# The projections and the FFN of a two-layer transformer as matmuls of 32 output columns, with the pace table searched anew

## The chip, the core and the metric

The kernel runs on one core of one Trainium2 chip. The metric is the device time of one execution in microseconds. The time before is 803.99 us, the median of 3 runs (803.82 to 804.15). The profile comes from one more execution with the hardware profiler on.

The engines that matter are TensorE (PE: matmuls into PSUM; PEld is its weight load), ScalarE (ACT: exponentials), VectorE (DVE) and GpSimd (POOL) for elementwise work, and SyncE (SP), which issues most of the DMAs.

## What is computed

Two blocks, each applied twice with the same weights, to x of 1 x 2048 x 448 in bf16. Block A is softmax attention with 16 heads of 28 columns, block B a feed-forward network with a squared relu.

```python
def _A_ref(x, wqkv, wo):
    B, S, D = x.shape
    H = 16; Dh = D // H
    qkv = (x @ wqkv).reshape(B, S, 3, H, Dh).transpose(2, 0, 3, 1, 4)
    q, k, v = qkv[0], qkv[1], qkv[2]
    scores = jnp.einsum("bhqd,bhkd->bhqk", q, k) * Dh ** -0.5
    p = _softmax(scores, axis=-1)
    o = jnp.einsum("bhqk,bhkd->bhqd", p, v)
    return o.transpose(0, 2, 1, 3).reshape(B, S, D) @ wo

def _B_ref(x, w1, b1, w2, b2):
    h = jnp.einsum("bsd,df->bsf", x, w1) + b1
    r = jnp.where(h > 0, h, 0)
    return jnp.einsum("bsf,fd->bsd", r * r, w2) + b2

x = A_x
x = x + _A_ref(_layernorm(x), A_wqkv, A_wo)
x = x + _B_ref(_layernorm(x), B_w1, B_b1, B_w2, B_b2)
x = x + _A_ref(_layernorm(x), A_wqkv, A_wo)
x = x + _B_ref(_layernorm(x), B_w1, B_b1, B_w2, B_b2)
```

The transposes are written here in plain form; the hidden width F is 1792.

## The kernel before

**Tiling.** The 448 columns of x stand in four chunks of 128 rows (the last is half zero). Each head is padded to 32 columns, so four heads make a group of 128 rows and 16 heads make four groups. Queries are worked off in blocks of 256 (two token tiles of 128); the last two blocks of the second layer have 128. Keys come in tiles of 128.

**Scores.** A score unit is one head's 512 scores per partition: two key tiles by 256 queries, or four by 128. There are 2048 units. A score group (`s_stream`, L1150) holds three units, each a matmul that uses 32 rows of PE and all 128 columns; units of different heads use different rows and run side by side. The group is written to one of two PSUM buffers of three banks (`sc`).

**Exponentials.** ACT takes a whole group with one instruction (`e_stream`, L1188). For some groups the third unit is taken away and given to DVE, so that ACT's instruction has two units (128 x 1024) in place of three (128 x 1536). DVE builds the exponential from bit operations in `a_unit`: a first pass at L1210 or L1212 that reads the scores. After L1210 the rest stays on DVE (L1228, L1232, L1235). After L1212 come three half passes (L1259, L1265, L1270), each on POOL or DVE, and a closing product on DVE (L1274).

**Value sums.** The exponentials of a key tile are multiplied by V (`p_stream`, L1376, and L1341 for units of DVE). These matmuls use all 128 rows of PE and 32 output columns, one head each; four heads, with four weight loads and four moving operands, run side by side into the four quarters of the partitions of one PSUM tile (`oT`).

**Projections and FFN.** All dense products go through one helper, `mm_tile`, with its matmuls at L805: K, Q and V (`qkv`), the output projection with `wo`, the hidden layer with `w1` and the FFN's output with `w2` (all three in `chain`). Each is a matmul of 128 rows by 128 output columns. The moving operand has N=256 columns (K, Q, `w1`), N=128 (the same for the blocks of 128 queries), N=448 (V, `wo`, `w2`), or N=320 and 128 at the very end. `mm_tile` cuts a tile's list of matmuls into operations of at most some 0.46 us (`MMC`), so that scores can come between. Each operation carries a mode, and `mm_tile` leaves it at its default, `"full"`.

**The order of the work.** The order on every engine is fixed when the program is built. `Planner.run` holds a list of streams with priorities, keeps a planned clock for every engine, and always emits the operation that can start first, scores ahead of other work. It counts 0.1 us when PE goes from one mode to another (row for scores, col for value sums, full for the rest):

```python
if e == "PE" and self.mode != o.mode:
    s = max(t, self.clock[e] + 0.1)
```

It also fills: a score group can be computed again (`again` in `s_stream`), and `heat` (L1625) adds matmuls whose result nobody reads, both when the planned load of PE over the last few microseconds is low (`HEAT`, `WINDOW`, `HOT`). The load is counted with a weight per mode:

```python
USE = {"row": 0.7, "col": 0.98, "full": 0.93}
```

**The pace.** Whether a group gives its third unit to DVE is decided in `apart`, by limits on DVE's planned load and backlog (`BUSY`, `LOW`, `TB`, `TB2` and others). `PACE` is a table that sets these and other planner constants anew when a given score group is reached, and `FORCE` and `SKIP` list groups that give the unit away, or don't, whatever the limits say.

Of the kernel before, what the change touches and what calls it, by code (L numbers as in the profile page):

```python
# [17 lines left out]
DHP = 32  # L18
G = 4
# [11 lines left out]
PLIM = 99.0  # L31
# [3 lines left out]
LADD = 0.15  # L35
NCELL = 9
RES = 2
RES2 = 4
XMIN = 4
HELD = 0.14  # L40
PWAIT = 3.0
# [52 lines left out]
NEAR = 3  # L94
# [17 lines left out]
AEND = 1  # L112
HOT = 0.9
MORE = 1
HEAT = 0.45
HWIN = 3.4
NEAR_U = 0
LASTP = 3.2
# [24 lines left out]
MMC = 0.46  # L143
VGAP = 0.03
QP = 6
FORCE = (22, 27, 31, 36, 64, 104, 108, 120, 122, 156, 162, 192, 196, 233, 235, 237, 254, 263, 287, 292, 301, 306,
         329, 341, 392, 408, 430, 445, 466, 501, 515, 553, 556, 567, 577, 593, 598, 602)
SKIP = (20, 29, 46, 135, 184, 195, 216, 222, 242, 262, 280, 282, 320, 321, 378, 388, 395, 404, 406, 409, 416, 418,
        433, 440, 446, 479, 500, 512, 526, 544, 574, 601, 609, 621, 622, 646, 652, 663)
PACE = {  # L150
    0: {'BUSY': 0.95, 'LOW': 0.7, 'CHUNK': 1, 'EV': 2.9, 'FAR': 6, 'KEEP': 5, 'LAG': 8, 'LEAD': 18, 'MARGIN': 3,
         'MORE': 3, 'PRE': 0.5, 'SLACK': 0.7, 'SPAN': 8, 'TB': 2.4, 'TB2': 2.4, 'V_AGE': 5, 'V_LAST': 3, 'V_PAST':
         2, 'C_PRIO': 1.6, 'V_PRIO': 4, 'V_LATE': 2.6, 'V_WAIT': 5, 'ASIDE': 1, 'XMIN': 4, 'HOLD': 6, 'LADD': 0.05,
         'RES': 2, 'RES2': 2, 'TASIDE': -0.2, 'EPRIO': 2.6, 'SPARE': 0, 'NEAR': 3, 'SOON': 1, 'VGAP': 0.03, 'PWAIT':
         0.3, 'PNEAR': 0.2, 'PORTP': 1, 'PLIM': 99.0},
    8: {'LEAD': 12, 'BUSY': 0.9, 'PLIM': 2},
    16: {'SPAN': 11},
    24: {'LAG': 3},
    32: {'PLIM': 2.6, 'EV': 3.5},
    40: {'TB2': 3.0},  # L160
    42: {'BUSY': 0.95, 'CHUNK': 3, 'EV': 2.9, 'LAG': 8, 'LEAD': 18, 'MORE': 1, 'SPAN': 8, 'TB': 1.6, 'TB2': 2.4,
         'V_PRIO': 8.5},
    56: {'BUSY': 1.0, 'LAG': 3},
    64: {'NEAR': 9, 'ASIDE': 0.2, 'LADD': 0.1},
    72: {'V_AGE': 4},
    88: {'V_AGE': 3},
    112: {'C_PRIO': 1.2, 'HOLD': 5},
    120: {'LEAD': 10, 'LAG': 12, 'SPARE': 3, 'ASIDE': 2},
    128: {'TB': 2.0, 'MORE': 3},
    136: {'PRE': 1.2, 'MARGIN': 6},  # L170
    144: {'EPRIO': 4},
    152: {'CHUNK': 1, 'VGAP': 0},
    160: {'BUSY': 0.95, 'V_PRIO': 4, 'V_PAST': 3},
    168: {'RES': 1, 'C_PRIO': 2.1, 'LOW': 1.0},
    176: {'EV': 2.2, 'TB2': 2.0, 'LOW': 0.5},
    192: {'PORTP': 0.3, 'SOON': 0.6},
    200: {'CHUNK': 2, 'PRE': 0.3},
    208: {'PNEAR': 0.25, 'V_AGE': 6},
    216: {'NEAR': 3},
    248: {'EPRIO': 6},  # L180
    256: {'ASIDE': 0},
    264: {'MARGIN': 10},
    280: {'PORTP': 2},
    288: {'HOLD': 6},
    296: {'TB': 1.0, 'PNEAR': 0.15},
    304: {'SPAN': 6},
    312: {'BUSY': 1.0},
    320: {'LEAD': 12, 'MARGIN': 6},
    328: {'V_LATE': 6},
    336: {'LOW': 1.0},  # L190
    360: {'PNEAR': 0.05, 'TB': 2.4, 'V_LATE': 2.6, 'V_AGE': 3},
    368: {'C_PRIO': 1.6},
    376: {'PNEAR': 0.15, 'V_PRIO': 8.5},
    384: {'XMIN': 3, 'LEAD': 18},
    392: {'CHUNK': 3},
    400: {'KEEP': 6, 'ASIDE': 4, 'V_AGE': 6, 'BUSY': 0.9},
    408: {'PWAIT': 0.6, 'MORE': 1},
    424: {'RES': 2, 'BUSY': 1.0},
    440: {'HEAT': 0.6, 'WINDOW': 3.4, 'CHUNK': 2},
    456: {'V_AGE': 5, 'TB': 1.3},  # L200
    480: {'TB': 1.6, 'PORTP': 0.3, 'PLIM': 2},
    488: {'LADD': 0.2, 'HOLD': 4},
    496: {'MARGIN': 3, 'PNEAR': 0.35},
    504: {'PWAIT': 0.3},
    512: {'KEEP': 4, 'EV': 2.9},
    520: {'V_AGE': 4, 'C_PRIO': 1.2, 'HOLD': 5},
    528: {'PRE': 0.8},
    536: {'XMIN': 4, 'SPAN': 15, 'ASIDE': 2, 'PRE': 0.3},
    544: {'V_AGE': 5, 'EV': 2.2},
    552: {'PORTP': 1, 'LEAD': 12, 'FAR': 17, 'PRE': 0},  # L210
    560: {'V_LATE': 6, 'VGAP': 0.03},
    568: {'SPARE': 0, 'NEAR': 9},
    576: {'SOON': 1.5, 'PNEAR': 0.15},
    584: {'PLIM': 1.3, 'LAG': 3, 'V_WAIT': 3},
    592: {'KEEP': 6, 'V_LAST': 2.2},
    600: {'V_AGE': 8},
    608: {'EV': 1.3, 'LOW': 0.8},
    616: {'PRE': 1.2, 'BUSY': 0.95, 'V_PAST': 2, 'FAR': 6},
    624: {'LADD': 0.1, 'BUSY': 0.9},
    648: {'PRE': 0.5, 'SPAN': 20, 'EV': 3.5, 'ASIDE': 0.2},  # L220
    656: {'ASIDE': 1, 'SLACK': 0.4},
    672: {'SOON': 1, 'ASIDE': 0.2},
    680: {'SLACK': 0.7},
}


# [180 lines left out]
def kernel(  # L407
# [205 lines left out]
    def pools_now(early=False):  # L613
        return (*R_m, R_sc) if early and ("s", LEND) not in pl.tok or len(s_left) == 0 else R_m
# [169 lines left out]
    def mm_tile(subs, evac, ev_dur, deps, any_engine=False, sets=(), early=False, post=(), acq=None, alone=0, seen=None, across=False):  # L784


        box = {}
        mms = [(c0, n, lhsT, rhs, i == 0, i == len(ops) - 1, own)
               for c0, n, ops in subs for i, (lhsT, rhs, *own) in enumerate(ops)]
        if across:  # L790
            mms = [mms[k * len(subs[0][2]) + i] for i in range(len(subs[0][2])) for k in range(len(subs))]
            mms = [(*m[:4], m is mms[0], m is mms[-1], m[6]) for m in mms]
        first = last = None
        i = 0
        while i < len(mms):
            dur, k = 0.003, i
            while k < len(mms) and (k == i or dur + mms[k][1] / 2400 < (0.6 if i == 0 and alone else MMC) and not (alone and k == alone)):
                dur += max(0.07, mms[k][1] / 2400 + 0.003)
                k += 1

            def fn(e, part=mms[i:k], i=i):
                if i == 0:
                    box["t"] = bank(first, "mt")
                for c0, n, lhsT, rhs, a, b, _ in part:
                    nc.tensor.matmul(box["t"][:, c0:c0 + n], lhsT=lhsT() if callable(lhsT) else lhsT, rhs=rhs,  # L805
                                     start=a, stop=b)
# [872 lines left out]
```

## Time and profile before

| | |
|---|---|
| median of 3 runs | 803.99 us (803.82 to 804.15) |
| the profiled execution | 804.07 us |
| its span, first to last instruction | 802.3 us |
| mean granted clock of PE | 1.000 |
| matmuls | 12234 |
| exponentials on ACT | 683 |

The span lies 1.8 us below the execution's own time; the rest is around the instructions. The profile's page has busy times, the chain that ended last, groups of instructions by line and the DMA queues. Besides the page, the trace answers with groups by shape, with waits (who waited for whom), with busy time by stretch, and with a timeline in which neighbouring instructions of one kind are merged: its columns are start and length in microseconds, engine, line, operation, tiles, shapes and count, and in brackets the idle time before. A matmul's recorded length holds its way through the array, so neighbouring matmuls overlap in the timeline; the distance of their starts is what they cost. "32\*128 32x256" means 32 rows and 128 columns of the array, a moving operand of 32 partitions and 256 columns.

### The profile page before, as it was taken

To read this page: it belongs to the slowest core of one execution; us is meant where nothing else is said; L and a number is where in the kernel's file an instruction comes from. 1 tells how busy PE (TensorE), PEld (TensorE's weight loads), DVE (VectorE), ACT (ScalarE), POOL (GpSimd) and SP (SyncE) were. 2 spreads that over 40 slices of the span, in tenths; PEclk is the share of its full clock that TensorE was granted. 3 is DMA by queue.
4 is the path that set the end of the run, shared out by engine and by line. 5 is a ranking of instruction groups with operands and counts; after the bars stand their busy time and mean duration, and the time that the engine had idled before them with its cause. 6 is when DMAs were issued, how large, how long until landed. Compare 5 with 4: busy or idle time off the path is not lost.

```text
span 802.3 us, 29224 instructions
## 1 busy us (share of the span) xinstructions
PE 779.4 (97%) x12234; PEld 417.7 (52%) x12234; DVE 744.6 (93%) x1818; ACT 789.6 (98%) x702; POOL 453.1 (56%) x715
## 2 busy tenths in 40 slices
PE   9999989999999999999999999989999999999998
PEld 6555545544555555555555545445454544546666
DVE  8999999999999999999999998999999999989554
ACT  9999999999999999999999999999999999999994
POOL 3446777657675664544566657667665576654100
PEclk9999999999999999999999999999999999999999
DMA  9300010000000000000000000011100000000000
GB/s 247 89 2 2 5 34 23 17 16 16 17 3 16 16 16 16 3 16 15 2 3 2 3 2 2 17 30 30 34 10 22 21 28 21 22 23 9 22 8 19
DMA packets 32336, 18.02 MB, mean 22 GB/s; under 512 B 17802, under 2 KB 31755, under 8 KB 32204
## 3 DMA queue, kind: packets, MB, share of 16 engines
q1 hardware_dynamic: 32060, 16.04, 7.3%
q8 instruction: 95, 1.56, 0.8%
q14 instruction: 37, 0.30, 0.1%
q10 hardware_dynamic: 144, 0.11, 0.0%
HBM read 13.87 MB, written 2.06 MB: 20 GB/s over the span
## 4 chain that ended last, share of the span: by engine, by line
PE 41%; ACT 31%; DVE 17%; issue 8%; DMA 1%; POOL 0%; SPq 0%; ACTq 0%; POOLq 0%; DVEq 0%
ACT pt L1188 31%; PE mt L805 19%; PE sc L1150 12%; PE oT L1376 7%; DVE pt L1212 3%; DVE r L1569 2%; PE oT L1341 1%; PE sc L805 1%; DVE V_sb L1576 1%; DVE pt L1210 1%; DVE v_c L1212 1%; DVE v_c L1274 1%; DVE K_sb L1274 1%; DVE x_sb L1509 1%; DVE K_sb L1212 1%
## 5 line engine op out<-in xcount | busy, mean ns | idle before, releaser
L1188 ACT ACTIVATE pt<-sc 128x1536 bf16<-128x1536 f32 (+1 forms) x683 | 776.8, 1289 | 1.2 <-PE sc L1150 0.9
L1150 PE MATMUL sc<-Q_sb,K_sb 32*128 32x256 bf16 (+1 forms) x4640 | 279.4, 265 | 15.9 <-ACT pt L1188 13.5
L1150 PEld LDWEIGHTS <-K_sb 32*128 32x128 bf16 x4640 | 100.9, 92 | 186.5 <-issue 118.5
L1376 PE MATMUL oT<-pt,V_sb 128*32 128x256 bf16 (+1 forms) x4000 | 167.7, 268 | 0.5 <-DVE Q_sb L824 0.3
L1376 PEld LDWEIGHTS <-V_sb 128*32 128x32 bf16 x4352 | 101.5, 96 | 45.3 <-issue 35.9
L805 PE MATMUL mt<-xnT,w 128*128 128x256 bf16 (+1 forms) x896 | 119.1, 271 | 0.9 <-DVE xnT L720 0.2
L1270 POOL TENSOR_SCALAR pt<-pt 128x512 int16<-128x512 int8 x131 | 84.2, 644 | 39.6 <-ACT pt L1188 5.7
L805 PEld LDWEIGHTS <-w 128*128 128x128 bf16 x952 | 78.0, 98 | 35.3 <-issue 26.6
L1212 DVE TENSOR_SCALAR pt<-sc 128x512 int16<-128x512 f32 x132 | 89.9, 684 | 2.3 <-PE sc L1150 1.6
L1569 DVE TENSOR_SCALAR r<-mt 128x512 bf16<-128x512 f32 (+1 forms) x107 | 73.1, 683 | 3.7 <-PE mt L805 3.2
L671 POOL TENSOR_TENSOR rstd<-mv,mhalf 128x2 f32<-128x2 f32 (+1 forms) x34 | 25.4, 748 | 79.2 <-DVE mv L674 72.7
L805 PE MATMUL mt<-w,V_sb 128*128 128x448 bf16 (+1 forms) x274 | 64.6, 348 | 0.0
L1270 POOL TENSOR_SCALAR v_c<-v_c 128x512 int16<-128x512 int8 x64 | 42.8, 668 | 24.5 <-DVE V_sb L1265 4.3
L1265 POOL TENSOR_SCALAR v_c<-pt 128x512 f16<-128x512 uint8 x57 | 38.1, 669 | 31.9 <-DVE K_sb L1259 5.8
L1509 DVE TENSOR_TENSOR x_sb<-x_sb,mt 128x448 bf16<-128x448 bf16 (+1 forms) x61 | 37.0, 607 | 13.2 <-PE mt L805 12.8
L1212 DVE TENSOR_SCALAR v_c<-sc 128x512 int16<-128x512 f32 x69 | 46.7, 683 | 0.7 <-PE sc L1150 0.6
L648 DVE BATCH_NORM_STATS2 st<-x_sb 128x6 f32<-128x448 bf16 x62 | 38.3, 619 | 0.6 <-DMA x_sb<-in_A_x_dram 0.5
L805 PEld LDWEIGHTS <-V_sb 128*128 128x128 bf16 x302 | 25.1, 98 | 24.9 <-issue 10.0
L1341 PE MATMUL oT<-v_c,V_sb 128*32 128x256 bf16 (+1 forms) x298 | 35.0, 273 | 0.0
L1270 POOL TENSOR_SCALAR K_sb<-K_sb 128x512 int16<-128x512 int8 x39 | 25.3, 649 | 11.2 <-DVE v_c L1274 2.5
L1265 POOL TENSOR_SCALAR K_sb<-pt 128x512 f16<-128x512 uint8 x35 | 23.9, 681 | 13.2 <-DVE pt L1212 4.3
L1576 DVE TENSOR_TENSOR V_sb<-r 128x512 bf16<-128x512 bf16 x70 | 29.2, 422 | 2.2 <-ACT r L1567 1.9
(217 smaller groups left out, 1257.4 us busy)
## 6 DMA issues: line engine op xcount, KB each, us to landing
rec<-scr SPq DMA_DIRECT2D x54, 128.0 KB
out_dram<-x_sb SPq DMA_DIRECT2D x15, 112.0 KB
x_sb<-in_A_x_dram SPq DMA_DIRECT2D x7, 224.0 KB
w<-in_B_w_dram SPq DMA_DIRECT2D x1, 1568.0 KB
w<-in_B_w_dram SPq DMA_DIRECT2D x1, 1344.0 KB
dn<-oT_sb SPq DMA_DIRECT2D x54, 4.0 KB
V_sb<-in_A_wqkv_dram SPq DMA_DIRECT2D x4, 168.0 KB
scr<-dn SPq DMA_DIRECT2D x27, 8.0 KB
```

The lines of the kernel that those rows point to most:

```text
L648: nc.vector.bn_stats(out=box["st"][:, :], in_=x_sb[:, t0 + j, :] if src is None else src())
L805: nc.tensor.matmul(box["t"][:, c0:c0 + n], lhsT=lhsT() if callable(lhsT) else lhsT, rhs=rhs, start=a, stop=b)
L1150: nc.tensor.matmul(dst[k][:, i * nt * P:(i + 1) * nt * P], lhsT=K_sb[l][rows, g, (kb + i) * P:(kb + i + 1) * P], rhs=Q_sb[rows, g, t0 * P: ...
L1188: t = nc.scalar.activation(out=pt[:, 0:n], in_=gbuf[gi]["sc"][:, 0:n], func=AF.Exp, scale=float(np.log(2.0)) * 2.0 ** -FRAC)
L1212: t = nc.vector.tensor_scalar(out=z.bitcast(DT.int16), in0=src, scalar1=2.0, scalar2=EXP_BIAS, op0=ALU.mult, op1=ALU.add)
L1265: on(e).tensor_scalar(out=box["f"], in0=gbuf[gi]["z"].bitcast(DT.uint8).rearrange("p (n t) -> p n t", t=2)[:, :, 0], scalar1=2.0 ** -9, sc ...
L1270: on(e).tensor_scalar(out=gbuf[gi]["z"].bitcast(DT.int16), in0=gbuf[gi]["z"].bitcast(DT.int8).rearrange("p (n t) -> p n t", t=2)[:, :, 1], ...
L1341: nc.tensor.matmul(box["t"][DHP * hh:DHP * hh + DHP, 0:n], lhsT=V_sb[l][:, kb + i, 4 * g + hh, :], rhs=gbuf[gi]["x2"][:, i * n:(i + 1) * n ...
L1376: nc.tensor.matmul(box["t"][DHP * hh:DHP * hh + DHP, 0:n], lhsT=V_sb[l][:, tb, 4 * g + hh, :], rhs=p, start=begin and j < G, stop=close an ...
L1509: nc.vector.tensor_tensor(out=x_sb[:, tb, lo:hi], in0=x_sb[:, tb, lo:hi], in1=t[:, 0:hi - lo], op=ALU.add)
L1569: nc.vector.tensor_scalar(out=r[:, 0:w], in0=t[:, 0:w], scalar1=0.0, scalar2=None, op0=ALU.max)
L1576: nc.vector.tensor_tensor(out=h[:, 0:w // n, :], in0=r, in1=r, op=ALU.mult)
```

## The change

The matmul in `mm_tile` becomes four, each with a quarter of the weight's columns and a quarter of the output's partitions, and the operation's mode becomes `"col"`:

```diff
                 for c0, n, lhsT, rhs, a, b, _ in part:
-                    nc.tensor.matmul(box["t"][:, c0:c0 + n], lhsT=lhsT() if callable(lhsT) else lhsT, rhs=rhs,
-                                     start=a, stop=b)
+                    w = lhsT() if callable(lhsT) else lhsT
+                    for c in range(G):
+                        nc.tensor.matmul(box["t"][DHP * c:DHP * c + DHP, c0:c0 + n],
+                                         lhsT=w[:, DHP * c:DHP * c + DHP] if len(w.shape) == 2 else w[:, c, :], rhs=rhs,
+                                         start=a, stop=b, tile_position=(0, DHP * c))
             own = list({d for m in mms[i:k] for d in m[6]})
             last = Op("PE", dur, fn, deps=(list(deps) if i == 0 else [last]) + own,
-                      acq=None if i else pools_now(early) if early else spare(len(mms)))
+                      acq=None if i else pools_now(early) if early else spare(len(mms)), mode="col")
```

`G` is 4 and `DHP` is 32. The planned length of an operation (`dur`) is not touched. Transposes and `heat` stay as they are.

Two constants and the pace are new. The tables `FORCE` and `SKIP` get other groups (29 and 26 in place of 38 and 38), and `PACE` other entries:

```diff
-WINDOW = 2.8
+WINDOW = 3.4
...
-HEAT = 0.45
+HEAT = 0.55
...
 PACE = {
-    0: {'BUSY': 0.95, 'LOW': 0.7, 'CHUNK': 1, 'EV': 2.9, 'FAR': 6, 'KEEP': 5, 'LAG': 8, 'LEAD': 18, 'MARGIN': 3,
-         'MORE': 3, 'PRE': 0.5, 'SLACK': 0.7, 'SPAN': 8, 'TB': 2.4, 'TB2': 2.4, 'V_AGE': 5, 'V_LAST': 3, 'V_PAST':
+    0: {'BUSY': 0.95, 'LOW': 0.7, 'CHUNK': 3, 'EV': 2.9, 'FAR': 6, 'KEEP': 5, 'LAG': 8, 'LEAD': 18, 'MARGIN': 3,
+         'MORE': 3, 'PRE': 0.5, 'SLACK': 0.7, 'SPAN': 8, 'TB': 3.4, 'TB2': 2.4, 'V_AGE': 5, 'V_LAST': 3, 'V_PAST':
...
-         'RES': 2, 'RES2': 2, 'TASIDE': -0.2, 'EPRIO': 2.6, 'SPARE': 0, 'NEAR': 3, 'SOON': 1, 'VGAP': 0.03, 'PWAIT':
+         'RES': 2, 'RES2': 2, 'TASIDE': 1, 'EPRIO': 2.6, 'SPARE': 0, 'NEAR': 3, 'SOON': 1, 'VGAP': 0.03, 'PWAIT':
...
-    8: {'LEAD': 12, 'BUSY': 0.9, 'PLIM': 2},
+    8: {'EV': 1.5, 'BUSY': 0.85, 'XMIN': 3},
...
```

As the planner decides all orders, the order on every engine is different behind the first groups of scores. Line numbers fall by 14 to 17: L805 becomes L790, L1150 L1136, L1188 L1174, L1376 L1362.

More of the change, by code (lines that the diff above doesn't have):

```diff
@@ L160 @@
[L160 to L201, printed above, removed]
@@ new lines @@
+    64: {'PLIM': 2, 'KEEP': 4},
+    80: {'C_PRIO': 1.2},
+    96: {'BUSY': 1.06, 'EV': 2.2},
+    104: {'V_PAST': 5},
+    112: {'LOW': 1.0},
+    128: {'RES2': 6, 'NEAR': 9},
+    136: {'NEAR': 3},
+    160: {'LOW': 0.5},
+    184: {'RES2': 4, 'MARGIN': 6},
+    192: {'V_LAST': 2.5},
+    200: {'VGAP': 0},
+    224: {'MARGIN': 10},
+    232: {'LAG': 12},
+    240: {'PNEAR': 0.35},
+    264: {'VGAP': 0.06},
+    272: {'VGAP': 0.15},
+    296: {'RES2': 2},
+    304: {'TASIDE': 0.2},
+    312: {'RES2': 6, 'V_LAST': 3},
@@ new lines @@
+    328: {'PORTP': 0},
+    336: {'PRE': 1.2},
+    344: {'SPARE': 3},
+    376: {'PNEAR': 0.25},
+    384: {'TASIDE': -0.2, 'FAR': 12},
+    400: {'NEAR': 9},
+    408: {'V_LAST': 2.5},
+    416: {'TASIDE': 0.2},
+    424: {'PORTP': 0.3, 'NEAR': 3},
+    440: {'CHUNK': 1},
+    464: {'VGAP': 0},
+    496: {'CHUNK': 2},
+    504: {'V_AGE': 8},
+    520: {'V_WAIT': 7, 'LOW': 0.7},
+    528: {'PRE': 0.3},
+    536: {'TB2': 0.9},
+    560: {'PLIM': 1.2},
+    568: {'V_LAST': 2.2},
+    576: {'LOW': 0.5},
```

45 lines of the change are left out of this document (16 added, 29 removed).

## The prediction

> **What bounds the kernel now.** I read the page first: the busy times, then the chain that ended last.
>
> ```profile
> PE 779.4 (97%) x12234; PEld 417.7 (52%) x12234; DVE 744.6 (93%) x1818; ACT 789.6 (98%) x702; POOL 453.1 (56%) x715
> ...
> PE 41%; ACT 31%; DVE 17%; issue 8%; DMA 1%; POOL 0%; SPq 0%; ACTq 0%; POOLq 0%; DVEq 0%
> ```
>
> No engine alone explains the time: ACT, PE and DVE are each over 90% busy, and the chain goes to and fro between them. So I cut the span into stretches and asked for the busy time of each. The columns are the stretch, its length, then busy microseconds and instructions of PE, PEld, DVE, ACT and POOL.
>
> ```profile
> 9.30:20.00 10.70, 10.70 (x104) 6.24 (x103) 10.53 (x30) 10.13 (x8) 1.68 (x4) 1.00 1.03 290
> 20.00:780.00 760.00, 741.71 (x11713) 391.09 (x11713) 719.75 (x1739) 759.38 (x671) 446.38 (x699) 1.00 0.06 17
> ...
> 787.30:802.30 15.00, 11.94 (x156) 9.34 (x153) 6.51 (x18) 4.84 (x9) 0.56 (x1) 1.00 0.06 17
> ```
>
> From 20 to 780 us ACT is busy 759.38 of 760.00 us: it works off exponentials without a pause, and the span is their sum plus about 9 us ahead of the first and 15 us behind the last. A change pays there if it takes exponentials from ACT, or loses if it makes one start late. How late they start now is in the waits (total us, times, longest):
>
> ```profile
> PE sc L1150 <- ACT pt L1188: 13.5, 31, 0.7
> ACT pt L1188 <- PE sc L1150: 0.9, 3, 0.5
> ```
>
> Of 683 score groups only 31 had to wait until ACT gave a buffer back. In all other places PE came to the scores from other work, so PE runs nearly as full as ACT and has little to give. ACT visibly waited three times. Small lateness is hidden in the recorded length of an exponential, so 0.9 us is a lower bound.
>
> **The change part by part.**
>
> *The exponentials left on ACT.* The pace decides which of the 2048 score tiles go to ACT and which to DVE. In the built order ACT has 345 exponentials of three tiles and 338 of two before, 341 and 342 after: 1711 tiles become 1707. The groups by shape give the price:
>
> ```profile
> L1188 ACT ACTIVATE pt<-sc 128x1536 bf16<-128x1536 f32 x345 | 489.7, 1501 | 0.6 <-PE sc L1150 0.5
> L1188 ACT ACTIVATE pt<-sc 128x1024 bf16<-128x1024 f32 x338 | 337.9, 1073 | 0.6 <-PE sc L1150 0.4
> ```
>
> The two differ by 1501 - 1073 = 428 ns, the cost of a tile; the number of instructions, and with it the fixed part, stays 683. Four tiles are 4 x 0.428 = 1.7 us less on an engine that has no pause. This lies wholly on the path: -1.7 us.
>
> *The four narrow matmuls.* Each of the 1254 matmuls of the projections and the FFN (L805) becomes four with 32 output columns. The shape with N=256 stands in the trace as the value sums (oT). First eight groups of four, then eight full matmuls, each up to the scores that follow (columns: start, length):
>
> ```profile
> 300.36 0.78 PEld L1376 LDWEIGHTS <-V_sb 128*32 128x32 bf16 x32 [0.21 <-issue]
> 300.36 0.28 PE L1376 MATMUL oT<-V_sb,V_sb 128*32 128x256 bf16 x1
> ...
> 300.37 0.28 PE L1376 MATMUL oT<-pt,V_sb 128*32 128x256 bf16 x1
> ...
> 300.48 0.27 PE L1376 MATMUL oT<-V_sb,V_sb 128*32 128x256 bf16 x1
> ...
> 301.35 0.40 PE L1150 MATMUL sc<-Q_sb,K_sb 32*128 32x256 bf16 x6
> ...
> 307.77 0.77 PEld L805 LDWEIGHTS <-w 128*128 128x128 bf16 x8 [0.21 <-issue]
> 307.78 1.05 PE L805 MATMUL mt<-xnT,w 128*128 128x256 bf16 x8
> ...
> 308.76 0.39 PE L1150 MATMUL sc<-Q_sb,K_sb 32*128 32x256 bf16 x6
> ```
>
> Thirty-two narrow weight loads and matmuls go from 300.36 to 301.35, 0.99 us; eight full ones from 307.78 to 308.76, 0.98 us. The four of a group start within 0.01 us (300.36 to 300.37), the next group 0.12 us after the first. So a group costs what one full matmul costs, and a whole block some 0.01 us more, because its fourth matmul starts that much later. With 438 blocks of such work in the new order this is at most 438 x 0.01 = 4.4 us of PE time, spread thin.
>
> N=128 also has its row: 64 narrow ones against 16 full ones.
>
> ```profile
> 781.39 0.90 PEld L1376 LDWEIGHTS <-V_sb 128*32 128x32 bf16 x64
> 781.39 1.08 PE L1376 MATMUL oT<-pt,V_sb 128*32 128x128 bf16 x64
> ...
> 787.64 0.90 PEld L805 LDWEIGHTS <-w 128*128 128x128 bf16 x16
> 787.64 1.07 PE L805 MATMUL sc<-xnT,w 128*128 128x128 bf16 x16
> ```
>
> The loads take 0.90 us in both, so they do not become the bound at the shortest N. [...]
>
> N=448 and N=320 in four narrow ones, all four reading one and the same moving operand, are in no row. From below: no gain per group is possible, since the columns stream at the pace that full and narrow ones already share. From above: each group pays the 0.01 us of stagger again because nothing overlaps it, 1254 x 0.01 = 12.5 us of PE time over all groups. I take zero beside the block's 0.01, since the row of N=256 is nearest, and keep the upper end for a rival.
>
> *The drains between shapes.* When PE goes over from one shape to another there is a gap:
>
> ```profile
> 108.36 0.12 PEld L1376 LDWEIGHTS <-V_sb 128*32 128x32 bf16 x8 [0.21 <-issue]
> 108.36 0.40 PE L1376 MATMUL oT<-pt,V_sb 128*32 128x256 bf16 x8
> 108.69 0.33 PEld L805 LDWEIGHTS <-wq 128*128 128x128 bf16 x4 [0.21 <-issue]
> 108.70 0.61 PE L805 MATMUL mt<-xnT,wq 128*128 128x256 bf16 x4
> 109.24 0.12 PEld L1150 LDWEIGHTS <-K_sb 32*128 32x128 bf16 x6 [0.21 <-DVE oT_sb L1401]
> ...
> 109.56 0.12 PEld L1376 LDWEIGHTS <-V_sb 128*32 128x32 bf16 x8 [0.21 <-issue]
> ```
>
> Four full matmuls from 108.70 reach the scores at 109.24: 0.54 us, of which eight of them in 0.98 us make 4 x 0.11 = 0.44, so a change of shape costs 0.10 us. Two groups of value sums, 0.22 us, take from 108.36 to 108.70 = 0.34: again about 0.1. After the change value sums and projections have one shape, and this gap between them goes. In the built order, changes of shape fall from 1349 to 1305: value sums now meet projections 84 times instead of 33, while transposes and warming matmuls, which stay full, gain a gap where they touch projections. 44 x 0.10 = 4.4 us less PE time. The gaps on both sides of the scores remain, since scores are tiled by rows.
>
> *PE filler.* The new order repeats 90 more score matmuls. Six take 0.32 us from 109.24 to 109.56, 0.22 without the gap, so 90 x 0.22 / 6 = 3.3 us; five of 30 warming matmuls go. Fillers are put where the planner sees room and are no need of the data. PE then has -4.4 + 4.4 + 3.3 = 3.3 us more to do at most, covered by the 760.00 - 741.71 = 18 us in which it is not busy between 20 and 780 us. Without that cover it costs those 3.3 us; with the block stagger hidden PE gains 4.4. Value taken: zero.
>
> *DVE and POOL.* DVE's first pass goes from 337 to 341. Of these, 90 instead of 67 stay on DVE to their end, in three passes, and 251 instead of 270 are closed with POOL's help; 156 half passes that DVE took over from POOL fall to 87.
>
> ```profile
> L1212 DVE TENSOR_SCALAR pt<-sc 128x512 int16<-128x512 f32 x132 | 89.9, 684 | 2.3 <-PE sc L1150 1.6 <-issue 0.2
> L1228 DVE TENSOR_SCALAR K_sb<-pt 128x512 int16<-128x512 int16 x12 | 3.4, 286 | 0.0
> L1232 DVE TENSOR_TENSOR K_sb<-pt,K_sb 128x512 bf16<-128x512 bf16 x12 | 5.4, 454 | 0.0
> L1235 DVE TENSOR_SCALAR pt<-pt 128x512 int16<-128x512 int16 x31 | 9.7, 317 | 0.2
> L1259 DVE TENSOR_SCALAR v_c<-pt 128x512 int16<-128x512 int16 x21 | 6.0, 286 | 0.0
> L1265 DVE TENSOR_SCALAR v_c<-v_c 128x512 f16<-128x512 uint8 x5 | 2.1, 423 | 0.0
> L1274 DVE TENSOR_TENSOR v_c<-v_c 128x512 bf16<-128x512 bf16 x63 | 26.4, 420 | 1.6 <-POOL v_c L1265 1.6
> L1270 POOL TENSOR_SCALAR pt<-pt 128x512 int16<-128x512 int8 x131 | 84.2, 644 | 39.6 <-ACT pt L1188 5.7 <-DVE v_c L1259 4.0 <-DVE K_sb L1274 2.8
> ```
>
> DVE: 4 x 0.684 + 23 x (0.286 + 0.454 + 0.317) - 42 x 0.286 - 27 x 0.423 - 19 x 0.420 = 2.7 + 24.3 - 12.0 - 11.4 - 8.0 = -4.4 us. POOL has 12 instructions more, 12 x 0.644 = 7.7 us, beside 453.1 busy of 802.3. ACT sheds tiles and DVE sheds time too, the work going to POOL, which has room. I count DVE's relief as nothing; it only makes a late result less likely.
>
> *Ends.* Ahead of the first scores the order of PE is the same. Behind the last exponential the same groups remain, with four fewer changes of shape and two new ones round the last transpose: -0.2 us, and some 0.2 of stagger. One relu more goes to ACT, which is idle there. Zero. PE's instructions rise from 24,470 to 37,978 rows:
>
> ```profile
> q8 instruction: 95, 1.56, 0.8%
> ```
>
> By that row 95 fetches become about 147, 1.2% of the DMA engines; the value sums already issue at the density of the new blocks. Zero, with some risk in the first 20 us, where the DMA share is about 1.
>
> *Sum.* The profiled execution took 804.07 us (span 802.3, 1.8 around it): 804.07 - 1.7 = 802.4. The median, 803.99, is 0.1 lower: **802.3 us**.
>
> **The rivals.**
>
> *PE's relief reaches the path.* If the 44 gaps count in full and the stagger is hidden: 803.99 - 1.7 - 4.4 = 797.9; at the chain's share of PE, 41%, 803.99 - 1.7 - 1.8 = 800.5. For it: only 31 waits on ACT, so PE is mostly the later one. Against: the fillers and more blocks eat it.
>
> *Each narrow group pays its stagger (slower).* Place: the FFN and value projections at N=448, whose shape no row shows. 12.5 us of PE time less 4.4 of gaps is 8.1; 41% of it 3.3: 803.99 - 1.7 + 3.3 = 805.6. In full, with the fillers of 3.3 on top, 813.7. It decides once the price per group passes about 0.007 us (4.4 + 1.7/0.41 = 8.5 us over 1254). For it: PE leads the chain. Against: eight groups with N=256 cost 0.01 us more, not 0.08.
>
> *The order is new and the gain is not kept.* The re-laid order may start some exponentials later by 1.7 us in all: 804.0. The wait row shows how little lateness is recorded now, 0.9 us, so there is more to lose than to win. In the same way losses of 3 us, 805.3, need only 0.004 us per exponential.
>
> [...]
>
> **How the numbers follow.** Chances: forecast 0.42, relief on the path 0.15, stagger 0.25, gain not kept 0.15, loads 0.03. A measurement of this kernel tells about 0.2%, 1.6 us, from no change, so faster means below 802.4. The forecast lies at that border: of its 0.42 I give 0.29 to faster and 0.13 to no change; the relief is faster. Stagger gives slower 0.24; gain not kept splits 0.08 no change, 0.07 slower; loads slower. Faster 0.44, no change 0.22, slower 0.34. The range leaves out the ends that need every price on the path: 797.9 below, and 808.5 above. The forecast's own range is 800.5 to 804.
>
> **What would show it.** Right: exponentials 341 and 342 at 1.50 and 1.07 us, ACT again over 99% busy from 20 to 780, eight narrow groups of L790 with N=256 in about 0.99 us up to the scores, N=448 groups 0.19 us apart, no 0.1 us gap between value sums and projections. Wrong: N=448 groups at 0.20 or more, score groups that ACT waits for in more than a few places, a granted clock below 1.0, PE idle with an issue wait in the first 20 us, or fewer microseconds of PE wait on ACT than 13.5 with a longer span.

## The result, and the profile after

| | before | changed |
|---|---|---|
| median (lowest to highest, runs) | 804.06 us (803.82 to 804.15, 4) | 813.81 us (813.16 to 815.60, 4) |
| ratio to before, 95% interval | | 1.0125 (1.0113 to 1.0138) |
| profiled execution, its span | 804.07, 802.3 us | 814.21, 812.4 us |
| end of the last exponential | 787.3 us | 793.4 us |
| stretch behind it | 15.0 us | 19.0 us |
| granted clock of PE | 1.000 | 0.998 (0.996 to 0.998 in the four runs) |

The change costs 9.8 us. The forecast was 802.3, in a range from 797.9 to 808.5. The last two lengths in the table already split the loss: about 6.1 us arise while ACT works off exponentials, 4.0 us behind the last one.

The page of the changed kernel, first its busy times, then the instruction queue, then the engines' shares of the chain that ended last:

```profile
PE 782.5 (96%) x18988; PEld 440.4 (54%) x18988; DVE 745.4 (92%) x1802; ACT 790.4 (97%) x703; POOL 464.7 (57%) x727
...
q8 instruction: 148, 2.42, 1.3%
...
PE 54%; ACT 27%; DVE 9%; issue 6%; DMA 2%; POOL 1%; SPq 0%; ACTq 0%; POOLq 0%; DVEq 0%
```

PE's busy time rose by 3.1 us and the chain runs over PE for 54% in place of 41%. The instruction queue carried 148 fetches in place of 95; 2.42 MB in 148 are 16 KB each. Spread over the fetches, PE's 37,978 rows are 257 for each, the 24,470 rows before 258.

The exponentials by shape:

```profile
L1174 ACT ACTIVATE pt<-sc 128x1536 bf16<-128x1536 f32 x341 | 489.6, 1489 | 4.3 <-PE sc L1136 3.9
L1174 ACT ACTIVATE pt<-sc 128x1024 bf16<-128x1024 f32 x342 | 345.7, 1061 | 2.3 <-PE sc L1136 1.6 <-POOL v_c L1251 0.4
```

They are 341 and 342, four tiles fewer, and still differ by 0.428 us. Taken one by one, an exponential of three tiles starts a usual 1.33 us ahead of the next, one of two tiles 0.90, in both kernels. By that the series itself is 1.7 us shorter. What the starts lose beyond this pace adds up to 13.2 us before and to 21.2 us now: exponentials start 8.0 us later in all. Of these, 2.6 us stand in one place at 513.3 us, 1.5 at 532.9 and 534.2, and 0.7 at 25.8. The other 3.2 are what is left when the spread lateness of the two kernels is subtracted, none of it over 0.8 us in one place. The larger pieces show as waits of ACT (total us, times, longest):

```profile
PE sc L1136 <- ACT pt L1174: 15.4, 39, 0.6
...
ACT pt L1174 <- PE sc L1136: 5.4, 7, 2.4
...
ACT pt L1174 <- POOL v_c L1251: 0.4, 1, 0.4
```

ACT visibly waited 5.8 us where it was 0.9, and one wait alone is 2.4. PE waited longer for ACT too (15.4 for 13.5): slack rose in some places while lateness rose in others.

PE's own waits show something that the profile before did not have at all, a matmul that waits for nothing but its issue:

```profile
PE sc L790 <- issue: 2.9, 2, 1.7
PE mt L790 <- issue: 0.7, 1, 0.7
PE oT L1362 <- issue: 0.7, 1, 0.7
```

The timeline of PE behind the last exponential shows where the first three of these stand:

```profile
793.92 0.83 PE L790 MATMUL sc<-xnT,w 128*32 128x128 bf16 x45
795.98 0.46 PE L790 MATMUL sc<-xnT,w 128*32 128x128 bf16 x19 [1.23 <-issue]
...
801.97 0.39 PE L790 MATMUL sc<-xnT,w 128*32 128x128 bf16 x13
804.02 1.35 PE L790 MATMUL sc<-xnT,w 128*32 128x128 bf16 x83 [1.66 <-issue]
...
805.48 1.58 PE L790 MATMUL mt<-w,V_sb 128*32 128x320 bf16 x37
807.76 0.86 PE L790 MATMUL mt<-w,V_sb 128*32 128x320 bf16 x19 [0.70 <-issue]
```

A run of 64 equal matmuls breaks off after 45, one of 96 after 13, and they go on 1.2 and 1.7 us later without a wait for data in the trace. Counted in the trace, 37057, 37569 and 37825 rows of PE (weight loads, matmuls and a few semaphore rows) stand ahead of these three breaks: 512 and 256 apart, about two fetches and one by the division above. In the first 20 to 30 us one more break of 0.66 us stands between value sums, at 24.89 us, behind 961 rows. All four counts are 193 above a multiple of 256. The exponential behind that first break waits 0.54 us.

The 2.4 us wait stands where layer two begins its attention. PE, DVE and ACT there:

```profile
508.74 0.61 PE L1136 MATMUL sc<-Q_sb,K_sb 32*128 32x256 bf16 x12
...
509.28 1.70 PE L790 MATMUL mt<-wv,xnT 128*32 128x448 bf16 x32
...
510.95 1.06 PE L790 MATMUL mt<-xnT,wk 128*32 128x256 bf16 x32
...
512.06 0.69 DVE L814 CAST K_sb<-mt 128x512 bf16<-128x512 f32 x1 [0.40 <-PE mt L790]
...
512.81 0.61 PE L1136 MATMUL sc<-Q_sb,K_sb 32*128 32x256 bf16 x12
...
513.31 1.45 ACT L1174 ACTIVATE pt<-sc 128x1536 bf16<-128x1536 f32 x1 [2.44 <-PE sc L1136]
```

The next scores need the last keys. The new order puts eight groups of value projections (1.7 us) ahead of the key projection, then come the projection and DVE's copy, and ACT has used up its two buffers long before.

The third place is in the clock. Stretches of the span (length, then PE, PEld, DVE, ACT, POOL, then granted clock, DMA share, GB/s):

```profile
520.00:530.00 10.00, 7.70 (x136) 4.12 (x135) 9.36 (x24) 10.00 (x11) 6.37 (x10) 1.00 0.15 37
530.00:534.00 4.00, 3.94 (x51) 1.56 (x48) 2.77 (x8) 3.08 (x3) 2.27 (x5) 0.57 0.17 52
534.00:544.00 10.00, 8.57 (x174) 4.42 (x174) 9.35 (x25) 9.80 (x9) 7.28 (x11) 1.00 0.11 31
```

From 530.2 to 533.6 us PE has half its clock, 0.50 granted over these 3.4 us. ACT, never idle in the ten microseconds before, is busy for 3.08 of these 4.

### The profile page after: what moved, and what is told of

Read it like the earlier page. It is cut to its first block, busy times and chain, and to the rows that moved or that the text cites. A ratio compares the mean times of both kernels' runs of the same rounds, so it can differ in the third digit from the quotient of the medians.

```text
span 812.4 us, 42665 instructions
## 1 busy us (share of the span) xinstructions
PE 782.5 (96%) x18988; PEld 440.4 (54%) x18988; DVE 745.4 (92%) x1802; ACT 790.4 (97%) x703; POOL 464.7 (57%) x727
## 3 DMA queue, kind: packets, MB, share of 16 engines
q8 instruction: 148, 2.42, 1.3%
## 4 chain that ended last, share of the span: by engine, by line
PE 54%; ACT 27%; DVE 9%; issue 6%; DMA 2%; POOL 1%; SPq 0%; ACTq 0%; POOLq 0%; DVEq 0%
ACT pt L1174 27%; PE mt L790 24%; PE sc L1136 16%; PE oT L1362 9%; PE oT L1327 2%; DVE pt L1198 1%; PE tp L691 1%; DMA rec<-scr 1%; PE sc L790 1%; DMA scr<-dn 1%; DVE r L1555 1%; DVE v_c L1198 1%; PE mt L1611 1%; DVE x_sb L1495 1%; DVE v_c L1260 0%
## 5 line engine op out<-in xcount | busy, mean ns | idle before, releaser
L1174 ACT ACTIVATE pt<-sc 128x1024 bf16<-128x1024 f32 (+1 forms) x683 | 777.5, 1275 | 6.6 <-PE sc L1136 5.4
L1136 PE MATMUL sc<-Q_sb,K_sb 32*128 32x256 bf16 (+1 forms) x4730 | 282.5, 265 | 17.9 <-ACT pt L1174 15.4
L1136 PEld LDWEIGHTS <-K_sb 32*128 32x128 bf16 x4730 | 103.0, 92 | 189.4 <-issue 124.7
L1362 PE MATMUL oT<-pt,V_sb 128*32 128x256 bf16 (+1 forms) x3936 | 167.6, 268 | 1.0 <-issue 0.7
L1362 PEld LDWEIGHTS <-V_sb 128*32 128x32 bf16 x4352 | 103.4, 96 | 41.4 <-issue 32.4
L790 PE MATMUL mt<-xnT,w 128*32 128x256 bf16 (+1 forms) x3584 | 121.9, 271 | 0.9 <-DVE xnT L703 0.5
L790 PEld LDWEIGHTS <-w 128*32 128x32 bf16 x3808 | 85.1, 96 | 32.7 <-issue 29.9
L1555 DVE TENSOR_SCALAR r<-mt 128x512 bf16<-128x512 f32 x106 | 72.7, 686 | 5.3 <-PE mt L790 4.6
L790 PE MATMUL mt<-w,V_sb 128*32 128x448 bf16 (+1 forms) x1152 | 72.5, 352 | 0.7 <-issue 0.7
L1198 DVE TENSOR_SCALAR pt<-sc 128x512 int16<-128x512 f32 x101 | 69.0, 684 | 4.4 <-PE sc L1136 4.1
L790 PEld LDWEIGHTS <-V_sb 128*32 128x32 bf16 x1208 | 29.0, 96 | 22.8 <-issue 10.8
L1327 PE MATMUL oT<-v_c,V_sb 128*32 128x256 bf16 x310 | 40.0, 275 | 0.0
L790 PE MATMUL mt<-wo,oTn 128*32 128x448 bf16 x496 | 31.5, 355 | 0.2 <-DVE x_sb L1495 0.2
L1198 DVE TENSOR_SCALAR K_sb<-sc 128x512 int16<-128x512 f32 x44 | 29.9, 682 | 1.8 <-PE sc L1136 1.7
```

The source lines that it names most:

```text
L790: nc.tensor.matmul(box["t"][DHP * c:DHP * c + DHP, c0:c0 + n], lhsT=w[:, DHP * c:DHP * c + DHP] if len(w.shape) == 2 else w[:, c, :], rhs=rhs,
L1136: nc.tensor.matmul(dst[k][:, i * nt * P:(i + 1) * nt * P], lhsT=K_sb[l][rows, g, (kb + i) * P:(kb + i + 1) * P], rhs=Q_sb[rows, g, t0 * P: ...
L1174: t = nc.scalar.activation(out=pt[:, 0:n], in_=gbuf[gi]["sc"][:, 0:n], func=AF.Exp, scale=float(np.log(2.0)) * 2.0 ** -FRAC)
L1198: t = nc.vector.tensor_scalar(out=z.bitcast(DT.int16), in0=src, scalar1=2.0, scalar2=EXP_BIAS, op0=ALU.mult, op1=ALU.add)
L1327: nc.tensor.matmul(box["t"][DHP * hh:DHP * hh + DHP, 0:n], lhsT=V_sb[l][:, kb + i, 4 * g + hh, :], rhs=gbuf[gi]["x2"][:, i * n:(i + 1) * n ...
L1362: nc.tensor.matmul(box["t"][DHP * hh:DHP * hh + DHP, 0:n], lhsT=V_sb[l][:, tb, 4 * g + hh, :], rhs=p, start=begin and j < G, stop=close an ...
```

## The experiments

Every kernel here ran beside the kernel before on the same chip; ratios are to those runs, whose medians were 804.01 to 804.23. "Tail" is the stretch behind the last exponential in the profiled execution.

| kernel | median us | ratio, 95% interval | tail us |
|---|---|---|---|
| new order, full matmuls | 812.50 | 1.0099 (1.0082 to 1.0115) | 15.0 |
| old order, narrow | 811.60 | 1.0096 (1.0069 to 1.0123) | 18.5 |
| changed, full behind the last scores | 810.47 | 1.0076 (1.0061 to 1.0091) | 15.0 |
| changed, 64 columns behind the last scores | 810.82 | 1.0094 (1.0077 to 1.0110) | 15.1 |
| old order, narrow up to the last scores | 807.50 | 1.0046 (1.0031 to 1.0061) | 15.0 |
| narrow, planned with the old pace | 846.73 | 1.0530 (1.0513 to 1.0547) | 30.5 |
| old kernel, 267 small matmuls more | 808.25 | 1.0051 (1.0036 to 1.0066) | 15.0 |
| old order, narrow only behind value sums | 805.64 | 1.0017 (1.0007 to 1.0026) | 15.0 |
| changed, full at both ends | 812.43 | 1.0117 (1.0085 to 1.0149) | 15.0 |
| the same, warming doubled | 811.06 | 1.0088 (1.0073 to 1.0103) | 14.9 |
| the same, no repeated scores | 808.27 | 1.0057 (1.0042 to 1.0072) | 15.0 |
| old kernel, no repeated scores | 804.87 | 1.0009 (1.0000 to 1.0019) | 15.0 |
| changed, full tail, last keys ahead of values | 823.25 | 1.0246 (1.0230 to 1.0261) | 19.5 |

### The order alone, and the shape alone

The new order with the full matmul:

```diff
-                    for c in range(G):
-                        nc.tensor.matmul(box["t"][DHP * c:DHP * c + DHP, c0:c0 + n],
...
+                    nc.tensor.matmul(box["t"][:, c0:c0 + n], lhsT=lhsT() if callable(lhsT) else lhsT, rhs=rhs,
+                                     start=a, stop=b)
```

> The changed kernel's order on every engine, instruction for instruction, but each dense product as one full matmul again. Theory A (PE runs dry of instructions where narrow matmuls stand dense): the three gaps behind the last exponential, 1.23 + 1.66 + 0.70 us in the changed kernel's timeline, and the one of 0.66 us at 24.9 us go, so about 813.8 - 4.3 = 809.5. Theory B (the loss is in the new order alone): 813 to 815, and the gaps in the tail stay. Theory C (the narrow shape costs time all over): 803 to 805, back to the time before.

The kernel before with the four narrow matmuls in its own order:

```diff
-                    nc.tensor.matmul(box["t"][:, c0:c0 + n], lhsT=lhsT() if callable(lhsT) else lhsT, rhs=rhs,
-                                     start=a, stop=b)
+                    w = lhsT() if callable(lhsT) else lhsT
+                    for c in range(G):
+                        nc.tensor.matmul(box["t"][DHP * c:DHP * c + DHP, c0:c0 + n],
...
+                                         start=a, stop=b, tile_position=(0, DHP * c))
```

> The old kernel's order on every engine, instruction for instruction, with each dense product as four narrow matmuls. Theory A: about 804.0 + 4.3 = 808.3, with gaps of over 0.5 us on PE behind the last exponential. Theory B: 803 to 804.5, as PE has fewer changes of shape. Theory C: 812 to 815.

Both are slower than before, by 8.3 and 7.4 us at 812.50 and 811.60 where the whole change costs 9.8, so the two parts do not add: each brings a loss of its own. The new order keeps its late exponentials with full matmuls; in its profile the waits of ACT are nearly the same,

```profile
ACT pt L1171 <- PE sc L1133: 5.5, 7, 2.5
```

and its last exponential ends at 796.1, 2.7 us later than in the changed kernel. Part of that is its clock in this execution, 0.996. Its order is that of the changed kernel, so the exponentials can be compared one by one. At 25 us its own start 0.7 us earlier: that is what the first break costs. From there to 520 us, with the full clock in both, the changed kernel gains 1.6 us. The tail is 15.0 us. The old order with the narrow shape has the longer tail, and the same breaks in it:

```profile
796.52 0.24 PE L807 MATMUL sc<-xnT,w 128*32 128x128 bf16 x4 [0.45 <-issue]
...
804.28 1.31 PE L807 MATMUL mt<-xnT,w 128*32 128x128 bf16 x80 [1.35 <-issue]
...
808.03 1.72 PE L807 MATMUL sc<-w,V_sb 128*32 128x320 bf16 x44 [1.43 <-issue]
```

Counted as above, 36801, 37313 and 37569 rows stand ahead of these breaks, again 193 above a multiple of 256. The breaks belong to the shape, the wait at layer two's start to the order. (This profiled execution, 815.11 us, had a granted clock of 0.949; the other three runs had 1.000 and took 809.99 to 812.68.)

### The tail

In the changed kernel, the full matmul once no scores are left, and the same in the old order with narrow matmuls before that:

```diff
                     w = lhsT() if callable(lhsT) else lhsT
+                    if not s_left:
+                        nc.tensor.matmul(box["t"][:, c0:c0 + n], lhsT=w, rhs=rhs, start=a, stop=b)
+                        continue
                     for c in range(G):
```

> The changed kernel, but dense products that PE gets behind the last score group are full matmuls again; the order is the changed kernel's. Theory A: the stretch behind the last exponential falls from 19.0 to about 15.0 us, the time to 809.8. Theory B: no change, 813.8, since the order is the same. Theory C: less than 0.5 us, as only some 130 of the 1254 groups go back.

> The old kernel's order, dense products as four narrow matmuls up to the last score group and full ones behind it. With the tail's gaps gone (the narrow tail was 18.6 us in place of 15.0), what is left against the kernel before is what the narrow shape costs beside the score groups. Theory D (a block between two score groups ends 0.01 us later, some 400 blocks, and PE's lateness reaches ACT): 806 to 808.5. Theory E (nothing but the instruction supply): 804 to 805.

The tail's stretch in the first of the two:

```profile
794.05:809.00 14.95, 12.05 (x153) 8.86 (x150) 6.09 (x17) 5.10 (x11) 0.56 (x1) 1.00 0.06 17
```

4.0 us of tail are back, and the time fell by 3.3. All four runs of this kernel had a clock of 1.000 and took 809.93 to 810.90 us; the one run of the new order with full matmuls that had it took 811.37. So beside the exponentials of this order the narrow shape gains some 0.5 to 1.4 us, by one run of the full form. Up to the last scores this kernel and the changed one are the same program, and compared one by one two things differ in their exponentials. With the full clock two exponentials, at 532.9 and 534.2 us in the changed kernel, follow the ones ahead of them 1.4 us sooner: that is what the half clock cost. And 1.5 us more than in the changed kernel are lost at breaks, of which two stand ahead of the tail, in dense value sums with N=128. The wait on issue in that profile, and one of its places:

```profile
PE oT L1365 <- issue: 2.3, 3, 1.1
```

```profile
780.88 0.68 PE L1365 MATMUL oT<-pt,V_sb 128*32 128x128 bf16 x35 [0.96 <-issue]
```

That break stands behind 36033 rows, 193 above a multiple of 256 once more. At the same row of the changed kernel 0.35 us lie between two starts, with the weight loads idle for 0.30 and the matmuls for 0.13: the place is the same, the length of a break is not.

In the old order the tail is back as well (807.50 after 811.60), and 3.4 us over the kernel before remain. There ACT waits eight times, 3.1 us in all, for scores, and breaks are left:

```profile
PE sc L1156 <- issue: 1.4, 2, 1.0
```

They are 1.00 us at 25.73, behind 961 rows, and 0.40 at 751.84; one of 0.46 follows at 779.08. In this execution, the slowest of its four at 809.43, the last exponential starts 5.6 us later than before. Compared one by one with the kernel before, whose order is the same, the exponentials start 0.2 us later from the first one on, fall back by 1.1 us up to the first break's end, and by 0.5 and 0.7 around the other two. Another 1.8 us are lost between 520 and 576 us; there DVE waits 1.4 us at 534.4 for a transfer over DRAM (`rec<-scr`), and behind it PE waits 0.6 us for DVE and ACT 0.7 us for PE. The remaining 1.1 us, between 28 and 520, are spread. So this kernel is not free of breaks, and the 3.4 us are not the price of the shape beside the exponentials alone.

Two explanations fit so far: PE runs out of instructions, or column tiles in themselves are slow at N=128. Two matmuls of 64 columns in the tail tell them apart, with column tiles but half as many instructions:

```diff
+                    if not s_left:
+                        for c in range(2):
+                            nc.tensor.matmul(box["t"][64 * c:64 * c + 64, c0:c0 + n],
...
+                                             rhs=rhs, start=a, stop=b, tile_position=(0, 64 * c))
+                        continue
```

> The changed kernel, but dense products behind the last score group are two matmuls of 64 output columns instead of four of 32: half the instructions of the narrow tail, still tiled by columns. Theory A (instruction supply): the stretch behind the last exponential is about 15.0 us, at most one short gap, 810.5. If tiling by columns itself makes the tail slow: 17 to 19 us, 812 to 814.

```profile
793.70:808.80 15.10, 12.31 (x286) 9.59 (x280) 6.09 (x17) 5.10 (x10) 0.56 (x1) 1.00 0.06 18
```

286 matmuls take 15.1 us, 153 took 14.95, 548 took 19.0. No break is left in it, with 32 of its matmuls at N=128 in 0.89 us, four instructions in 0.056. So the breaks come with the number of instructions per microsecond, which also fits their places, 256 rows or a multiple of it apart.

### The pace

Narrow matmuls and the planner's new mode, with `FORCE`, `SKIP`, `PACE`, `WINDOW` and `HEAT` of before:

```diff
-WINDOW = 3.4
+WINDOW = 2.8
...
-HEAT = 0.55
+HEAT = 0.45
```

> The changed kernel's narrow matmuls and its planner mode, with FORCE, SKIP, PACE, WINDOW and HEAT of the kernel before; the planner lays the order anew. If the new pace fits the new shape: slower than the changed kernel, over 815. If the pace is no better than the old one: 806 to 812, with no wait of over 2 us on ACT near 510 us. Theory A: in both cases the stretch behind the last exponential is about 19 us.

846.73 us, with one wait of ACT of 14.9 us, which ends at 523.8, again where layer two begins, and a tail of 30.5. Once operations carry another mode, the planner lays another order, and the old tables no longer fit it. With the new tables the time is 813.81: they repair most of what the mode breaks, and not all of it.

### What PE's time is worth

A matmul of 64 columns whose result is overwritten, ahead of 267 tiles of the kernel before:

```diff
+            if s_left:
+                nc.tensor.matmul(box["t"][:, 0:64], lhsT=ident[:, :], rhs=xns[0][:, 0:64], start=True, stop=True)
```

> The kernel before, full matmuls, with one more matmul of 64 columns ahead of the first one of each dense tile up to the last score group; its result is overwritten. 267 times about 0.03 us is 8 us of PE time, spread over the span. It measures what such time costs. If ACT's stock of scores hides it: 804 to 805. If it counts by PE's share of the chain, 41%: 807.5. If PE is the bound in full: 812.

4.1 us more. A full matmul with N=128 takes 0.056 us (the prediction's row, 16 in 0.90), so 267 of half the length are an estimated 7.5 us. About half of a PE microsecond reaches the end, close to the 41% that the prediction took from the chain.

The opposite, narrow matmuls in the old order only where PE comes straight from value sums, so that a gap goes and none is added (107 groups):

```diff
+                narrow = bool(s_left) and pl.was == "col"
...
+                    if not narrow:
+                        nc.tensor.matmul(box["t"][:, c0:c0 + n], lhsT=w, rhs=rhs, start=a, stop=b)
+                        continue
```

> The old kernel's order; a dense operation is narrow only where PE comes to it straight from value sums or from a narrow operation that follows them, and full in all other places, so the gap between the two shapes goes there and nothing else changes (107 groups are narrow). If a 0.1 us gap taken from PE reaches the end: about 25 gaps, 2.5 us of PE, times the 41% of the chain: 803.0 to 803.8. If such a gap is worth nothing where it stands: 804.2.

By half of 25 gaps of 0.1 us this should have gained some 1.2 us; it lost 1.5. Its profile has a wait that the kernel before has not:

```profile
DVE oTn L1510 <- DMA rec<-scr: 2.4, 3, 1.0
```

DVE waits for a round trip over DRAM, 2.4 us in all, for which it waits nowhere in the profile before. That this wait makes the loss was not tried: it stays open.

### Both ends, and the clock

The changed kernel with full matmuls until 110 of the 2048 score units have been given out, and again from 1850 on, so that neither the head nor the dense stretch before the tail can run out of instructions:

```diff
+                    if not 110 < at[0] < 1850:
+                        nc.tensor.matmul(box["t"][:, c0:c0 + n], lhsT=w, rhs=rhs, start=a, stop=b)
+                        continue
```

> The changed kernel's order; dense products are full matmuls while fewer than 111 or more than 1849 of the 2048 units are scored, and behind the last scores, and narrow in between. Against the run with a full tail alone the gaps on PE at 25 us and near 773 and 781 us (1.2, 0.5 and 1.1 us there) go too. Theory A: about 810.5 - 2 = 808.5. If these gaps were hidden: 810.5. What is left against the kernel before, some 4 us, then belongs to the order: the wait of 2.6 us near 510 us and small ones.

No wait on issue is left, yet the time scatters: 810.04 and 810.33 with a granted clock of 1.000, 814.54 and 815.83 with 0.993. To try whether more work on PE holds the clock, each warming matmul was then doubled:

```diff
-                    nc.tensor.matmul(t[:, 0:D], lhsT=ident[:, :], rhs=xns[0][:, 0:D], start=True, stop=True)
+                    for _ in range(2):
+                        nc.tensor.matmul(t[:, 0:D], lhsT=ident[:, :], rhs=xns[0][:, 0:D], start=True, stop=True)
```

> The changed kernel's order with full matmuls at both ends, as measured before at 810.0 to 815.8, and each warming matmul done twice. If the two runs of 814.5 and 815.8, whose granted clock was 0.993 in place of 1.000, lost their time to a clock drop where PE has too little work (520 to 545 us): all runs have a clock of 1.000 and 809.5 to 811. If the drop has another cause: clocks below 1.000 again and a spread of some 5 us.

The clock was 1.000 in all four runs, and they lie within 810.59 to 811.75. So the upper two values before, 4.4 to 5.6 us above the lower two, go with the clock; 7 us over the kernel before remain without it and without breaks. That the doubling held the clock is not shown by four runs, since two of four kept it without.

### The fillers

The same without repeated score matmuls (4352 in place of 4730), and the kernel before without its own (4352 in place of 4640):

```diff
-                for i in list(range(4)) * (again + 1):
+                for i in list(range(4)):
```

> The changed kernel's order with full matmuls at both ends and doubled warming matmuls (811.06), without the repeated score matmuls (the planner's filler; the scores are the same). About 378 matmuls go, some 14 us of PE time. If the new order loses in small pieces because fillers make PE late (a us of PE cost 0.5 us in the run with the small extra matmul): 805 to 808. If fillers stand only where PE would wait for ACT anyway: 810.5 to 811.5, or more where the granted clock drops. If the lateness is in the order of DVE and POOL: no change.

> The kernel before, without its repeated score matmuls (about 288, some 10 us of PE time). If they only fill waits: 804.0 with the granted clock at 1.000. If they make PE late as well: 800 to 803, faster than both kernels. If the clock needs them: a clock below 1.000 and over 806.

The new order gains 2.8 us by that, the old one loses 0.8, at the edge of what its interval tells. In the old order the fillers stand where PE would have waited for ACT anyway (17.5 us of such waits without them, 13.5 with); in the new one part of them makes exponentials late. In the new order without them ACT still waits 3.8 us for scores, 2.3 of it at the start of layer two.

### The last keys ahead of the values

The wait of 2.44 us should go if the last key projection is emitted ahead of the value projections:

```diff
-            yield from values()
-            yield from turned(*ks[-1])
+            if l == 1 and t0 == 14:
+                yield from turned(*ks[-1])
+                yield from values()
...
```

> The changed kernel with a full tail, and for the last token block of layer 1 the last key projection stands ahead of the value projections instead of behind them (1.5 us of PE work changes places with 1.0). From there on the planner lays the order anew; ACT gets 343 and 340 exponentials, two tiles more (+0.9 us). If the wait of 2.4 us on ACT near 513 us comes from that order: it falls to about 1, the time to 809.5 to 810. If the layer's chain is late for another reason: the wait stays and the time is 810.5 to 812.

At its place it did what it should. The timeline of ACT, then its waits:

```profile
511.89 5.14 ACT L1181 ACTIVATE pt<-sc 128x1536 bf16<-128x1536 f32 x4 [0.77 <-PE sc L1143]
```

```profile
ACT pt L1181 <- PE oT L1369: 8.2, 1, 8.2
ACT r L1560 <- PE sc L790: 5.0, 1, 5.0
```

2.44 us became 0.77. But the planner laid everything behind it anew, with one wait of 8.2 us from 572.6 on and a tail of 19.5, and the time rose by 12.8 against the same kernel without the edit. So the wait's place is shown, and its price at the end could not be measured by itself: the pace tables hold for one order only.

## Why the prediction was wrong, step by step

**The step that failed: the instruction supply.** Under *Ends* the prediction set the instruction supply at "Zero, with some risk in the first 20 us", because "the value sums already issue at the density of the new blocks". It went by the mean (1.2% of the DMA engines) and saw a risk at the head alone. Value sums stand between scores and transposes; behind the last scores nothing thins the stream. At N=128 a narrow group is eight instructions in 0.056 us, so 256 last 1.8 us, against 7.2 us for the full form's two per group. There PE stops, 1.2 and 1.7 us at a time, at rows 512 and 256 apart, where a fetch carries some 257 by the page. The tail grew by 4.0 us, all of which came back with full matmuls there, and all but 0.1 with half as many instructions; the head's break adds 0.7. The row of N=128 value sums in the prediction (64 in 0.90 us) was true and too short to show it: 128 instructions, half a fetch.

**A second step that failed: the lateness of the new order, left out of the sum.** The sum took 1.7 us off an engine "that has no pause" and added nothing for late exponentials, though by their usual pace those of the kernel before already start 13.2 us late in all. The rival "The order is new and the gain is not kept" was right in kind and too small: it was priced at 804.0 to 805.3, with up to three microseconds of lateness spread thin. The new order with full matmuls, free of the breaks, ran at 812.50. The spread part came near its price, 3.2 us in the changed kernel. What it missed is concentrated: 2.6 us in a single place at the start of layer two, where value projections stand ahead of the keys that the scores need, and what the clock adds. The prediction read that ACT waited only three times before, and did not look in the new order for the places where scores depend on a projection.

**The fillers, taken as covered.** "Value taken: zero", or 3.3 us without the cover. All repeats together cost 2.8 us in the new order (811.06 to 808.27) and gain 0.8 in the old. So the cover, 18 us in which PE is not busy, does not lie where all of the new order's fillers are.

**The granted clock.** It was named as a sign and given no price. In the profiled execution the half clock goes with ACT's waits of 0.84 us at 532.9 and 0.28 at 534.2, and cost 1.4 us against the same program at the full clock; in the kernel with full matmuls at both ends the runs with 0.993 took about 5 us more than those with 1.000.

**The stagger rival** came nearest in its number, 813.7 "in full", by a mechanism that did not occur. Its count of 1254 groups was also too low: the profile before has 2217 matmuls at L805, which makes its upper end 22 us of PE time. Groups with N=448 follow each other at 0.19 us, and the gap behind value sums is gone, as in these rows of PE's timeline:

```profile
173.81 0.40 PE L1362 MATMUL oT<-pt,V_sb 128*32 128x256 bf16 x8
174.04 0.36 PE L790 MATMUL mt<-w,V_sb 128*32 128x448 bf16 x4
174.23 0.36 PE L790 MATMUL mt<-w,h 128*32 128x448 bf16 x4
174.53 0.39 PE L1136 MATMUL sc<-Q_sb,K_sb 32*128 32x256 bf16 x6
```

Two groups of value sums from 173.81 to 174.04 are 0.23 us, two of 0.11 and nothing between; the next projection group follows 0.19 later.

**What was right.** The four tiles (-1.7 us) came as priced, and so did the narrow group's cost, the block's 0.01 us and the removed gaps; of the 4.4 us of gaps, less the blocks' part, 0.5 to 1.4 reached the end, by the new order's full and narrow forms at one clock. Narrow loads do not bind: no run shows the slower loads to which the forecast gives a chance of 0.03, and groups at N=128 keep 0.056 us in four narrow matmuls. The share of PE's time that reaches the end was 41% by the chain and about half by the 267 matmuls.

**The sum.** In the profiled executions the span grew by 10.2 us. The tail is 4.0 of these; the exponentials start 8.0 us later, of which 0.7 are the head's break, 2.6 the wait at layer two, 1.5 the places of the half clock and 3.2 spread; the four tiles give 1.7 back. That makes 10.3. The repeats' 2.8 us are part of the lateness, for all of them in a kernel without breaks. The parts are not independent, as the breaks at other places and the replanned order show: no run takes them away together.

What remains open is the spread lateness, and what the narrow shape is worth beside the exponentials: it gains about 1 us in the new order, and in the old one some 3.4 us are lost, of which breaks make a part. Waits of DVE on the DRAM round trip were seen in such kernels, but not taken away. No version that ran beats the kernel before.

## What to carry to other kernels

Splitting a matmul into column tiles cost no time for a group here (0.056 us at N=128, 0.19 at N=448) and multiplied the instructions: count the longest dense stretch in fetches (about 257 of PE's rows each here), and keep the full form where short moving operands run without anything between them, at the ends above all. A shape change that moves an automatic order is two changes: run the new order with the old instruction, and look in it for the places where the critical engine depends on a projection before pricing tiles. Fillers placed where a load estimate is low were free in the order for which that estimate had been tuned, and cost 2.8 us in the other.

## What the runs showed of the hardware

Where narrow matmuls stand dense, up to eight instructions in 0.056 us, PE stops for 0.4 to 1.7 us at places that are multiples of 256 of its instructions apart: in the changed kernel, the old order with narrow matmuls, and both of these with a full tail, all that were counted lie 193 rows above a multiple of 256. In the tail of 64-column matmuls, with four instructions in that time, no stop came. Few such places bring a stop: the changed kernel has 148 of them, and in five the issue of PE pauses for over 0.25 us. Nor is its length fixed: at row 36033, with the same instructions ahead of it, PE was idle for 0.96 us in the changed kernel with a full tail, and for 0.13 in the changed kernel itself.

PE's clock fell to half for 3.4 us (530.2 to 533.6) in the changed kernel's profile; PE had been busy 7.70 of the ten microseconds from 520 to 530 and never idle for more than 0.6 at once. The changed kernel with a full tail, the same program up to there, had a granted clock of 1.000 in all four runs, so the program alone does not decide it here. One execution of the old order with narrow matmuls had 0.949 over its whole span, three others 1.000; the cause of both is open.
